# 64x32 instead of 64x64 TensorE tiles in the chunked recurrence of a gated linear attention with an MLP behind it

## The chip, the cores and the metric

The kernel runs on one core of one Trainium2 chip. The metric is the device time of one launch in microseconds (us). Before the change three runs gave 178.33, 179.40 and 180.58 us; the median is 179.4 us. The engines are TensorE (PE in the profile; PEld are its weight loads), VectorE (DVE), ScalarE (ACT), GpSimd (POOL) and SyncE (SP), which only issues DMAs here.

## The reference

Inputs are q, k, v and alpha of shape (4 batches, 8 heads, 768 steps, 48 features), and two weights, 384 x 2048 and 2048 x 384.

```python
for t in range(S):                       # per batch and head, state is D x D
    state = alpha[:, :, t, :, None] * state + np.einsum('bhd,bhe->bhde', k[:, :, t], v[:, :, t])
    y[:, :, t] = np.einsum('bhd,bhde->bhe', q[:, :, t], state)
x = y.transpose(0, 2, 1, 3).reshape(B * S, H * D)      # 3072 x 384
h = x @ w_in
r = np.maximum(h, 0.0)
out = (r * r) @ w_out                                  # 3072 x 384
```

## The kernel before, in words

**Tiling.** The 768 steps of a batch are cut into three pairs of chunks, 256 steps a pair and 128 a chunk, so there are 12 pairs, g = 0 to 11. On the partitions a chunk lies as 64 rows of two neighbouring steps (index i or n). Features are padded from 48 to 64 a head, and heads go two by two, so a head pair fills 128 partitions of a transposed tile.

**Stages of a pair.** (1) `loads`: four transfers, alpha, k, q, v, into RAW. (2) `decay` (`decay_half` for the first two pairs): logarithms on ScalarE, running sums over the chunk on TensorE (L502 and L504; L541 and L546 for the first two pairs), exponentials, and the scaled k and q in bf16 (QKS) on VectorE. `values` casts v to bf16 (VBF), on GpSimd for the first two pairs. (3) `turned`: QKS is transposed to QKT, on TensorE for the first three pairs, by a DMA on SyncE's queue from there on. (4) `scores` (L634): 32 matmuls of 64x64 tiles, 128 columns each, in two halves of 16; VectorE multiplies them by the causal mask into PMB (L644, four instructions). (5) `carry` (L663): the end states of the pair's chunks, k times v, 32 matmuls of 48 columns (16 in the last pair of a batch, where one chunk is enough). VectorE and GpSimd make the state behind each chunk of it (L678, L681, L683, tile SBF). (6) `mixed` (L702): the values, 48 matmuls of 128 columns (PMB times VBF), and the part that comes from the states, in two halves of 12 (6 in the first pair of a batch). The second half waits until the first has left the array (`drain`), because both add into the same bank from other row groups. ScalarE copies the result to XT (L740). (7) `up` (L757): eight units of 6 matmuls, 256 columns each; ScalarE applies the relu (L761), VectorE squares (L763). (8) `down` (L781): eight groups of 4 matmuls with 384 columns, then a copy by ScalarE (L788) and an output DMA; the last chunk goes in two halves of columns (L801, L806).

**Tiles on TensorE.** `scores`, `carry` and `mixed` use a quarter of the array for a matmul: 64 rows (the chunk's row half or the head's half) by 64 columns (which half of the output partitions). In `mixed` the 384 output features are cut into six groups of 64; each of the 8 heads with 48 features touches one or two of them, which gives the list `shares` of 12 pieces. The order of the matmuls goes round the four quarters.

**Order.** Nothing is issued in program order. `Program.add` records each operation with an engine, an estimated duration in ns, what it reads and writes, and a due time `at`; `form` is the tile shape of TensorE work. `order` plays the program through with these durations and gives each engine the ready operation with the earliest due time; TensorE prefers work of the form that it is in, and a change of form is reckoned with 95 ns. `fill` puts warm-up matmuls (L770) into idle time of TensorE that this plan shows ahead of the first down matmul. `plan` places semaphore waits. The due times are 2 g plus an offset for each stage, from the tables OFF, EARLY (pairs 0 and 1) and MID (pair 2). SyncE holds the loads, the transposes and the outputs in one queue, in the order of the plan; GpSimd's queue holds the casts of the first two pairs, the weights' DMAs (four for w_in, which wait for alpha of pair 1, then four for w_out) and the states' second step.

## Time and profile before

| what | value |
|---|---|
| median of three runs | 179.4 us (178.33 to 180.58) |
| span of the profiled execution | 177.0 us |
| granted TensorE clock | 0.999 |
| L757 up, PE | 576 matmuls, busy 74.0 us |
| L781 down, PE | 368 matmuls, busy 71.4 us |
| L702 mixed, values, PE | 576 matmuls of 64x64 tiles, busy 10.4 us |
| L702 mixed, from the states, PE | 240 matmuls, busy 8.6 us |
| L634 scores, PE | 384 matmuls, busy 8.0 us |
| L663 end states, PE | 320 matmuls, busy 5.5 us |
| L770 warm-up, PE | 22 matmuls, busy 7.6 us |

The span runs from the first to the last instruction of the profiled execution; the runs' times hold 2.4 us more at the median. Busy time of a matmul reaches to its modelled end, and these ends overlap with the next starts, so the price of a group is read from start to start. A row of the timeline has start, duration to the end of its last instruction, engine, line, operation, tiles, shape, count and, in brackets, idle time of the engine before it with what ended it. A row of a windows table has the window, its length, busy time and count of each engine (where TensorE alone was asked for, only its own), the granted clock, the mean share of the 16 DMA engines and GB/s. Of the DMA queues, `q8 instruction` are transfers of instructions.

### The profile page before, as it was taken

How to read it: one execution, taken by the hardware profiler on the slowest of the kernel's cores; microseconds unless marked ns; L12 is line 12 of the kernel's file. 1: busy time of each engine (PE TensorE's matmuls, PEld its weight loads, DVE VectorE, ACT ScalarE, POOL GpSimd, SP SyncE). 2: the span in 40 equal slices, each digit the busy share in tenths (PEclk: the TensorE clock that was granted, in tenths of full speed). 3: DMA queues.
4: the chain of work that ended last, by engine and by line, in shares of the span. 5: the costliest groups of instructions: out<-in, count | busy, mean ns of one | idle time of the engine just before them, and what ended most of it. 6: DMA issues, size and time to landing. Idle time of an engine off the chain costs nothing.

```text
span 177.0 us, 6054 instructions
## 1 busy us (share of the span) xinstructions
PE 169.4 (96%) x2648; PEld 123.8 (70%) x2648; DVE 117.1 (66%) x251; ACT 116.8 (66%) x235; POOL 19.3 (11%) x35
## 2 busy tenths in 40 slices
PE   7989699999999989999999999999999999999993
PEld 2656568776666877787777777777777777767772
DVE  7998534599889797993896694875663952732400
ACT  4764376695894878796989779756566645455531
POOL 4179400001100201001002001001001010000000
PEclk9999999999999999999999999999999999999999
DMA  5999999899999999999899999831701331101112
GB/s 137 308 298 171 193 204 216 228 302 275 269 216 298 198 285 240 277 248 240 222 325 214 282 232 279 202 84 50 167 4 44 92 75 44 48 4 52 37 44 93
DMA packets 75994, 31.85 MB, mean 180 GB/s; under 512 B 69184, under 2 KB 75968, under 8 KB 75968
## 3 DMA queue, kind: packets, MB, share of 16 engines
q1 hardware_dynamic: 72256, 28.32, 64.1%
q0 software_dynamic: 3712, 3.15, 11.7%
q8 instruction: 21, 0.34, 0.8%
q14 instruction: 5, 0.04, 0.1%
HBM read 25.17 MB, written 4.72 MB: 169 GB/s over the span
## 4 chain that ended last, share of the span: by engine, by line
PE 76%; DMA 14%; SPq 4%; ACT 3%; issue 2%
PE psH L757 32%; PE psO L781 30%; PE psG L702 6%; DMA qkt<-qks 4%; DMA win<-in_moe_w_in_dram 4%; SPq L474 4%; DMA raw<-in_v_dram 3%; DMA raw<-in_alpha_dram 3%; PE psG L634 3%; PE psO L801 1%; PE psG L663 1%; ACT xt L740 1%; ACT rr L761 1%; PE psG L502 1%; PE psG L574 1%
## 5 line engine op out<-in xcount | busy, mean ns | idle before, releaser
L761 ACT ACTIVATE rr<-psH 128x512 bf16<-128x512 f32 x96 | 56.6, 598 | 35.9 <-PE psH L757 34.9
L757 PE MATMUL psH<-xt,win 128*128 128x256 bf16 x576 | 74.0, 273 | 0.7 <-DMA win<-in_moe_w_in_dram 0.3
L781 PE MATMUL psO<-wout,gt 128*128 128x384 bf16 x368 | 71.4, 326 | 0.0
L757 PEld LDWEIGHTS psH<-xt,win 128*128 128x128 bf16 x576 | 54.5, 98 | 14.4 <-ACT rr L761 1.4
L763 DVE TENSOR_TENSOR gt<-rr 128x512 bf16<-128x512 bf16 x96 | 39.9, 423 | 36.0 <-ACT rr L761 35.4
L781 PEld LDWEIGHTS psO<-wout,gt 128*128 128x128 bf16 x368 | 34.5, 98 | 17.1
L644 DVE TENSOR_TENSOR pm<-psG,mask 128x512 bf16<-128x512 f32 x48 | 30.8, 685 | 1.6 <-PE psG L634 1.5
L523 DVE TENSOR_TENSOR qks<-raw,asb 128x768 bf16<-128x768 f32 x20 | 18.6, 956 | 6.5 <-ACT asb L512 6.5
L683 POOL TENSOR_TENSOR sbf<-ust,acp 128x192 bf16<-128x192 f32 x16 | 9.3, 579 | 119.1 <-DVE ust L681 119.0
L740 ACT ACTIVATE xt<-psG 128x384 bf16<-128x384 f32 x24 | 13.1, 597 | 5.7 <-PE psG L702 5.7
L788 ACT ACTIVATE osb<-psO 128x384 f32<-128x384 f32 x23 | 11.3, 493 | 4.8 <-PE psO L781 4.3
L493 DVE TENSOR_TENSOR raw<-raw 128x384 f32<-128x384 f32 x20 | 11.0, 555 | 2.4 <-DMA raw<-in_alpha_dram 1.7
L512 ACT ACTIVATE asb<-psG 128x384 bf16<-128x384 f32 x20 | 9.8, 490 | 1.6 <-PE psG L504 1.4
L702 PEld LDWEIGHTS psG<-pm,vbf 64*64 64x64 bf16 x576 | 8.4, 107 | 2.8 <-issue 1.4
L702 PE MATMUL psG<-pm,vbf 64*64 64x128 bf16 x576 | 10.4, 218 | 0.0
L702 PE MATMUL psG<-qkt,sbf 64*64 64x128 bf16 x240 | 8.6, 220 | 1.4 <-issue 1.4
L485 ACT ACTIVATE vbf<-raw 128x768 bf16<-128x768 f32 x10 | 8.4, 843 | 1.1 <-DMA raw<-in_v_dram 1.0
L634 PEld LDWEIGHTS psG<-qkt 64*64 64x64 bf16 x384 | 5.9, 106 | 4.4 <-issue 1.4
L770 PE MATMUL psO<-warm 128*128 128x512 bf16 x22 | 7.6, 472 | 1.1 <-DVE warm L391 1.1
L634 PE MATMUL psG<-qkt 64*64 64x128 bf16 x384 | 8.0, 219 | 0.5 <-DMA qkt<-qks 0.4
L681 DVE TENSOR_TENSOR ust<-psG,sbf 128x192 f32<-128x192 f32 x15 | 5.3, 356 | 2.8 <-POOL sbf L683 2.3
L702 PEld LDWEIGHTS psG<-qkt,sbf 64*64 64x64 bf16 x240 | 5.2, 106 | 2.7 <-issue 2.6
(65 smaller groups left out, 99.9 us busy)
## 6 DMA issues: line engine op xcount, KB each, us to landing
raw<-in_k_dram SPq DMA_DIRECT2D x12, 384.0 KB, 5.0
raw<-in_q_dram SPq DMA_DIRECT2D x12, 384.0 KB, 5.6
raw<-in_v_dram SPq DMA_DIRECT2D x12, 384.0 KB, 5.4
out_dram<-osb SPq DMA_DIRECT2D x23, 192.0 KB, 3.5
raw<-in_alpha_dram SPq DMA_DIRECT2D x11, 384.0 KB, 5.2
win<-in_moe_w_in_dram POOLq DMA_DIRECT2D x4, 384.0 KB, 8.7
wout<-in_moe_w_out_dram POOLq DMA_DIRECT2D x4, 384.0 KB, 12.3
raw<-in_alpha_dram SPq DMA_DIRECT2D x2, 192.0 KB, 2.7
```

The costliest lines, as they stand in the source:

```text
L493: add("DVE", lambda e: e.tensor_tensor(dst, a0, a1, ALU.mult), 470, at_, reads=reads, writes=writes)
L512: add("ACT", lambda act, z=z: act.activation(ASB[a][:, z, 0, :], ps[:, 0:HD], AF.Exp, scale=2.0 * z - 1.0), 372, at + 0.04 + 0.02 * z, rea ...
L523: add("DVE", lambda dve, z=z, decays=decays: dve.tensor_tensor(QKS[x][:, z, :, :, 0:D], both(r, z), decays, ALU.mult), 870, at + 0.05 + 0. ...
L634: last = pe.matmul(banks[i, j // 2][0][64 * c:64 * c + 64, col:col + 128].rearrange("p (a b) -> p a b", a=2), QKT[t][64 * i:64 * i + 64, 0 ...
L644: add("DVE", lambda dve, i=i, X=X, ps=ps: dve.tensor_tensor(PMB[m][:, i, 2 * X:2 * X + 2].rearrange("p j n s -> p j (n s)"), ps[:].rearran ...
L702: last = pe.matmul(o, lhsT, rhs, start=(c, n % 2) not in begun, stop=True, skip_group_check=True)
L740: add("ACT", lambda act, ps=ps, base=base: act.activation(XT[:, :, base:base + C].rearrange("f k (p i) -> f k i p", i=2), ps[:, 0:HD].rear ...
L757: last = pe.matmul(ps[:, f * TW:(f + 1) * TW], WIN[:, kt, fj * 128:(fj + 1) * 128], XT[:, kt, g * TW:(g + 1) * TW], start=(kt == 0), stop= ...
L761: add("ACT", lambda act: act.activation(RR[r][:], ps[:], AF.Relu), 480, at, reads=[key], writes=[key, ("rr", r)])
L763: add("DVE", lambda dve: dve.tensor_tensor(gt[:, 2 * u:2 * u + 2, :], rr, rr, ALU.mult), 340, at, reads=[("rr", r)], writes=[("gt", g % NG ...
L781: last = pe.matmul(ps[:, 0:DM], GT[g % NGT][:, fj, tt * 128:(tt + 1) * 128], WOUT[:, fj, :], start=(fj == 0), stop=(fj == FT - 1))
L788: add("ACT", lambda act: act.activation(OSB[o][:], ps[:, 0:DM], AF.Copy), 372, at, reads=[key], writes=[key, ("osb", o)])
```

## The change

Values, the part from the states, and the end states use 64x32 tiles: 64 rows by 32 columns, eight to the array. The 384 output features are cut into twelve groups of 32 (16 pieces in `shares`), so the values take 64 matmuls, each half of the part from the states 16 (8), and the end states 64 (32). Scores keep 64x64. The planner's durations change with it, it gets a model of the arrival of instructions (blocks of 256; the next block comes 4300 ns after a block's start in the first 30 us, and 2700 ns after a point 48 instructions ahead of it later), and the offsets of the stages are new, with a table each for pairs 0 and 1. With these the order on every engine is another. TensorE gets 3246 matmuls where it had 2648; the other engines' instructions are the same in number and kind.

In the new order TensorE has, in the early part: pair 0's decay and transposes, half of its scores, its end states, pair 1's decay, the other half of the scores, 11 warm-up matmuls, pair 0's values and first half from the states, pair 1's end states, the second half, a warm-up matmul, pair 1's transposes, two up units, half of pair 1's scores, an up unit, the other half, three up units, pair 1's values. Before, pair 1's scores stood ahead of the first up unit and its end states behind the second. On VectorE two of pair 0's four masks stand behind pair 1's scaled k and q; before, all four stood ahead. On SyncE, from pair 3 on, a transpose stands ahead of the next pair's alpha load, and the first output ahead of k, q and v of pair 4.

```diff
+CFG = {'OFF': {'decay': -4.835, 'turned': -3.891, 'scores0': -2.056, 'scores1': -2.206,
+               'carry': -3.164, 'mixed': -1.691, 'up': -1.026},
...
+ 'CW': 32}
...
+    OTHER = 20
+    BLOCK, QUEUE, FETCH, FETCH_LATE, BUSY_UNTIL = 256, 48, 4300.0, 2700.0, 30000.0
...
+            if e == "PE" and op.mm:
+                each, began = op.work / op.mm, t
+                for i in range(op.mm):
+                    x = count + i
+                    lead = 0 if t < self.BUSY_UNTIL else self.QUEUE
+                    if (x + lead) % self.BLOCK == 0:
+                        b = (x + lead) // self.BLOCK + 1
+                        came[b] = t + i * each + (self.FETCH if t < self.BUSY_UNTIL else self.FETCH_LATE)
+                    if x % self.BLOCK == 0 and came.get(x // self.BLOCK, 0.0) > t + i * each:
+                        late = came[x // self.BLOCK] - t - i * each
...
+        W = CFG.get("CW", 64)
+
         def mm(pe):
             for j in range(NP):
                 for n in range(2):
-                    for i in range(2):
-                        for c in chunks:
-                            last = pe.matmul(banks[c][0][64 * i:64 * i + 64, j * D:(j + 1) * D],
-                                             QKS[x][64 * c:64 * c + 64, 0, n, 2 * j + i, :],
+                    for d in range(0, 64, W):
+                        for i in range(2):
+                            for c in chunks:
+                                last = pe.matmul(banks[c][0][64 * i + d:64 * i + d + W, j * D:(j + 1) * D],
+                                                 QKS[x][64 * c:64 * c + 64, 0, n, 2 * j + i, d:d + W],
...
-        add("PE", mm, 170 + 150 * len(chunks), at, reads=[("qks", x, 0, X) for X in range(2)] + [("vbf", vb)],
-            writes=[b[1] for b in banks], form=64)
+        add("PE", mm, 250, at, reads=[("qks", x, 0, X) for X in range(2)] + [("vbf", vb)],
+            writes=[b[1] for b in banks], form=W, mm=1024 // W * len(chunks))
...
-    shares = [(h, n, 64 * n - D * h) for h in range(H) for n in range(2 * KT) if -64 < 64 * n - D * h < D]
+    NG = HD // 32
+    shares = [(h, n, 32 * n - D * h) for h in range(H) for n in range(NG) if -32 < 32 * n - D * h < D]
...
-            o = banks[c][0][64 * (n % 2):64 * (n % 2) + 64, n // 2 * 128:n // 2 * 128 + 128]
+            o = banks[c][0][32 * (n % 4):32 * (n % 4) + 32, n // 4 * 128:n // 4 * 128 + 128]
...
-            order = [[s for s in shares if s[1] % 2 == col] for col in range(2)]
-            for y in range(2 * KT):
+            order = [[s for s in shares if s[1] % 4 == col] for col in range(4)]
+            for y in range(4):
                 for i in range(2):
-                    for col in range(2):
+                    for col in range(4):
                         h, n, off = order[col][y]
...
-        add("PE", mm, 640, at, reads=[("vbf", vb)] + [("pm", m, i, X) for i in range(2) for X in range(2)],
-            writes=[b[1] for b in banks], form=64)
+        add("PE", mm, 455, at, reads=[("vbf", vb)] + [("pm", m, i, X) for i in range(2) for X in range(2)],
+            writes=[b[1] for b in banks], form=32, mm=64)
...
-        o = EARLY if g < FIRST else MID if g < TURN else OFF
+        o = EARLY[g] if g < FIRST else MID if g < TURN else OFF
```

More of the change, by code (lines that the diff above doesn't have):

```diff
@@ L1 @@
 import heapq
+CFG = {'OFF': {'decay': -4.835,
+         'turned': -3.891,
+         'scores0': -2.056,
+         'scores1': -2.206,
+         'carry': -3.164,
+         'mixed': -1.691,
+         'up': -1.026},
+ 'MID': {'decay': -4.897,
+         'turned': -3.845,
+         'scores0': -3.102,
+         'scores1': -3.012,
+         'carry': -3.319,
+         'mixed': -1.513,
+         'up': -1.423},
+ 'E0': {'decay': -6.997,
+        'turned': -5.74,
+        'scores0': -5.321,
+        'scores1': -3.593,
+        'carry': -3.833,
+        'mixed': -3.228,
+        'up': -1.919},
+ 'E1': {'decay': -6.326,
+        'turned': -4.764,
+        'scores0': -3.707,
+        'scores1': -3.627,
+        'carry': -5.044,
+        'mixed': -2.649,
+        'up': -2.169},
+ 'CW': 32}
 import concourse.bass as bass
@@ L25, in __init__ @@
         self.count = None
+        self.mm = 0
         self.signal = False
@@ L52, in add @@
     def add(self, eng, fn, work, at, reads=(), writes=(), dma=None, nbytes=0, rate=0.0, behind=None, form=None,
-            drain=None):
+            drain=None, mm=0):
         op = Op(len(self.ops), eng, fn, work, at, dma, nbytes, rate)
@@ L79, in add @@
         op.form = form
+        op.mm = 2 * mm
         self.ops.append(op)
@@ L94, in order @@
         self.sequence = []
+        self.stalls = []
         known = dict.fromkeys((o.n for o in self.ops), 0.0)
@@ L150, in order @@
         form = None
+        count, came = 64 + self.OTHER, {}
         while left:
@@ L193, in order @@
                 form = op.form
+            if e == "PE" and op.mm:
[8 more added lines that the diff above has]
+                        late = came[x // self.BLOCK] - t - i * each
+                        self.stalls.append((t + i * each, late))
+                        if i:
+                            op.work += late
+                            each = op.work / op.mm
+                        else:
+                            t += late
+                count += op.mm
             free[e] = t + op.work
@@ L434, in bass_gla_recurrent__then__act_relu_squared_kernel @@
     OPENS = {2: 5}
+    RUNS, OPENS = CFG.get("RUNS", RUNS), CFG.get("OPENS", OPENS)
     pieces = [(w, n) for w in ("in", "out") for n in range(WH)]
@@ L506, in sums @@
             return last
-        add("PE", sums, 265, at + 0.02, reads=lab + ["hinc"], writes=[key])
+        add("PE", sums, 265, at + 0.02, reads=lab + ["hinc"], writes=[key], mm=1 + NP)
         add("ACT", lambda act: act.activation(heads(RO[o_][:]), odd, AF.Ln), 412, at + 0.03,
@@ L549, in sums @@
             return last
-        add("PE", sums, 430, at + 0.01, reads=[("lab", l, X), "hinc", "hexc"], writes=[key])
+        add("PE", sums, 430, at + 0.01, reads=[("lab", l, X), "hinc", "hexc"], writes=[key], mm=8)
         for z in range(2):
@@ L575, in tr @@
                 return last
-            add("PE", tr, 450, at + 0.02 * z, reads=[("qks", x, z, X) for X in range(2)] + ["ident"], writes=[key])
+            add("PE", tr, 450, at + 0.02 * z, reads=[("qks", x, z, X) for X in range(2)] + ["ident"], writes=[key], mm=8)
             dst = QKT[t][:, z].rearrange("p i j s -> p (i j s)")
@@ L608, in tr @@
                 return last
-            add("PE", tr, 225, at + 0.02 * z, reads=[("qks", x, z, X), "ident"], writes=[key])
+            add("PE", tr, 225, at + 0.02 * z, reads=[("qks", x, z, X), "ident"], writes=[key], mm=4)
             if g > 0 and z == 0:
@@ L640, in scores @@
         add("PE", mm, 112 * len(js), at, reads=[("qkt", t, z, X) for z in range(2) for X in halves],
-            writes=[b[1] for b in banks.values()], form=64)
+            writes=[b[1] for b in banks.values()], form=64, mm=8 * len(js))
         mask = bass.AP(tensor=MASK, offset=0, ap=[[256, 128], [0, 2], [1, 256]])
@@ L660, in mm @@
                 for n in range(2):
-                    for i in range(2):
-                        for c in chunks:
-                            last = pe.matmul(banks[c][0][64 * i:64 * i + 64, j * D:(j + 1) * D],
-                                             QKS[x][64 * c:64 * c + 64, 0, n, 2 * j + i, :],
-                                             VBF[vb][64 * c:64 * c + 64, n, 2 * j + i, 0:D],
-                                             start=n == 0, stop=n == 1)
-            return last
-        add("PE", mm, 170 + 150 * len(chunks), at, reads=[("qks", x, 0, X) for X in range(2)] + [("vbf", vb)],
-            writes=[b[1] for b in banks], form=64)
+                    for d in range(0, 64, W):
[3 more added lines that the diff above has]
+                                                 QKS[x][64 * c:64 * c + 64, 0, n, 2 * j + i, d:d + W],
+                                                 VBF[vb][64 * c:64 * c + 64, n, 2 * j + i, 0:D],
+                                                 start=n == 0, stop=n == 1)
+            return last
+        add("PE", mm, 250, at, reads=[("qks", x, 0, X) for X in range(2)] + [("vbf", vb)],
+            writes=[b[1] for b in banks], form=W, mm=1024 // W * len(chunks))
         for c in chunks:
@@ L698, in one @@
         def one(pe, c, n, lhsT, rhs):
-            o = banks[c][0][64 * (n % 2):64 * (n % 2) + 64, n // 2 * 128:n // 2 * 128 + 128]
+            o = banks[c][0][32 * (n % 4):32 * (n % 4) + 32, n // 4 * 128:n // 4 * 128 + 128]
             if len(rhs.shape) == 3:
                 o = o.rearrange("p (a b) -> p a b", a=2)
-            last = pe.matmul(o, lhsT, rhs, start=(c, n % 2) not in begun, stop=True, skip_group_check=True)
-            begun.add((c, n % 2))
+            last = pe.matmul(o, lhsT, rhs, start=(c, n % 4) not in begun, stop=True, skip_group_check=True)
+            begun.add((c, n % 4))
             return last
         def before(pe, swap):
-            order = [[[s for s in shares if s[0] % 2 == i and s[1] % 2 == col] for col in range(2)] for i in range(2)]
-            for y in range(KT):
-                for col in range(2):
+            order = [[[s for s in shares if s[0] % 2 == i and s[1] % 4 == col] for col in range(4)] for i in range(2)]
+            for y in range(2):
+                for col in range(4):
                     for i in range(2):
@@ L715, in before @@
                             at_ = D + PAD * (h // 2) + off
-                            last = one(pe, c, n, SBF[(2 * g + c) % NS][64 * i:64 * i + 64, at_:at_ + 64],
+                            last = one(pe, c, n, SBF[(2 * g + c) % NS][64 * i:64 * i + 64, at_:at_ + 32],
                                        QKT[t][64 * i:64 * i + 64, 1, :, h // 2, 64 * c:64 * c + 64])
@@ L720, in mm @@
         def mm(pe):
-            order = [[s for s in shares if s[1] % 2 == col] for col in range(2)]
-            for y in range(2 * KT):
+            order = [[s for s in shares if s[1] % 4 == col] for col in range(4)]
+            for y in range(4):
                 for i in range(2):
-                    for col in range(2):
+                    for col in range(4):
                         h, n, off = order[col][y]
@@ L727, in mm @@
                         for c in range(2):
-                            last = one(pe, c, n, flat[64 * c:64 * c + 64, PAD * h + off:PAD * h + off + 64],
+                            last = one(pe, c, n, flat[64 * c:64 * c + 64, PAD * h + off:PAD * h + off + 32],
                                        PMB[m][64 * c:64 * c + 64, h % 2, h // 2, i, :])
             return last
-        add("PE", mm, 640, at, reads=[("vbf", vb)] + [("pm", m, i, X) for i in range(2) for X in range(2)],
-            writes=[b[1] for b in banks], form=64)
+        add("PE", mm, 455, at, reads=[("vbf", vb)] + [("pm", m, i, X) for i in range(2) for X in range(2)],
+            writes=[b[1] for b in banks], form=32, mm=64)
         reads = [("qkt", t, 1, X) for X in range(2)] + [("sbf", (2 * g + c) % NS) for c in chunks]
         keys = [banks[c][1] for c in chunks]
-        first = add("PE", lambda pe: before(pe, 0), 80 * len(chunks), at + 0.004, reads=reads, writes=keys, form=64)
-        add("PE", lambda pe: before(pe, 1), 80 * len(chunks), at + 0.008, reads=reads, writes=keys, form=64, drain=first)
+        first = add("PE", lambda pe: before(pe, 0), 57 * len(chunks), at + 0.004, reads=reads, writes=keys, form=32, mm=8 * len(chunks))
+        add("PE", lambda pe: before(pe, 1), 57 * len(chunks), at + 0.008, reads=reads, writes=keys, form=32, drain=first, mm=8 * len(chunks))
         for c in range(2):
@@ L759, in mm @@
             return last
-        add("PE", mm, 655, at, reads=[("xt", 2 * g), ("xt", 2 * g + 1), ("win", 2 * u * WH // FT)], writes=[key])
+        add("PE", mm, 655, at, reads=[("xt", 2 * g), ("xt", 2 * g + 1), ("win", 2 * u * WH // FT)], writes=[key], mm=6)
         add("ACT", lambda act: act.activation(RR[r][:], ps[:], AF.Relu), 480, at, reads=[key], writes=[key, ("rr", r)])
@@ L771, in busy @@
         return last
-    add("PE", lambda pe: busy(pe, 7), 2950, -6, reads=["warm"], writes=[("psO", i) for i in range(NPO)])
+    add("PE", lambda pe: busy(pe, 7), 2950, -6, reads=["warm"], writes=[("psO", i) for i in range(NPO)], mm=7)
     def down(g, tt, p, at):
@@ L784, in down @@
         op = add("PE", mm, 650, at, reads=[("gt", g % NGT, f) for f in range(4 * p, 4 * p + 4)] + [("wout", 4 * p * WH // FT)],
-                 writes=[key])
+                 writes=[key], mm=4)
         downs.append(op)
@@ L804, in last_down @@
                 add("PE", mm, 330, at + c + 0.25 * p, reads=[("gt", (G - 1) % NGT, f) for f in range(4 * p, 4 * p + 4)]
-                    + [("wout", 4 * p * WH // FT)], writes=[key])
+                    + [("wout", 4 * p * WH // FT)], writes=[key], mm=4)
             add("ACT", lambda act, ps=ps, o=o: act.activation(OSB[o][:, 0:HW], ps[:, 0:HW], AF.Copy), 215, at + c + 0.75,
@@ L814, in bass_gla_recurrent__then__act_relu_squared_kernel @@
     MID = dict(decay=-4.614, turned=-4.532, scores0=-3.642, scores1=-3.538, carry=-4.386, mixed=-1.189, up=-1.023)
-    stages = [(2 * r[0] + (EARLY["decay"] + 0.5 if run else 0.96 - 2 * NRAW), lambda at, run=run: weights(at, run))
+    for d, name in ((OFF, "OFF"), (EARLY, "EARLY"), (MID, "MID")):
+        d.update(CFG.get(name, {}))
+    EARLY = [{**EARLY, **CFG.get("E%d" % i, {})} for i in range(FIRST)]
+    stages = [(2 * r[0] + (CFG["WAT"][run] if "WAT" in CFG else EARLY[1]["decay"] + 0.5 if run else 0.96 - 2 * NRAW), lambda at, run=run: weights(at, run))
               for run, r in enumerate(RUNS)]
     for g in range(G):
-        o = EARLY if g < FIRST else MID if g < TURN else OFF
+        o = EARLY[g] if g < FIRST else MID if g < TURN else OFF
         stages.append((2 * g - 2 * NRAW + 0.95, lambda at, g=g: loads(g, at)))
```

## The prediction

> **What bounds the kernel now.** I read the page's busy shares and its chain first, then the timeline of TensorE (PE) in a steady stretch, then PE's idle time.

> ```profile
> span 177.0 us, 6054 instructions
> PE 169.4 (96%) x2648; PEld 123.8 (70%) x2648; DVE 117.1 (66%) x251; ACT 116.8 (66%) x235; POOL 19.3 (11%) x35
> PE 76%; DMA 14%; SPq 4%; ACT 3%; issue 2%
> ...
> 174.03 0.33 ACT osb L806
> ```

> PE is busy for 96% of the span, no other engine for more than 66%, and the chain is mostly PE. So the end is PE's last matmul (174.0 us, where the last copy starts), and a step is worth what it adds to PE's stream or takes from it. Rows of matmuls give their price by the distance between starts, since the modelled ends overlap:

> ```profile
> 75.49 1.47 PE L757 MATMUL psH<-xt,win 128*128 128x256 bf16 x12
> 76.80 0.81 PE L781 MATMUL psO<-wout,gt 128*128 128x384 bf16 x4
> 77.45 1.47 PE L757 MATMUL psH<-xt,win 128*128 128x256 bf16 x12
> 78.86 0.86 PE L702 MATMUL psG<-pm,vbf 64*64 64x128 bf16 x48
> 79.55 0.34 PE L702 MATMUL psG<-qkt,sbf 64*64 64x128 bf16 x12
> 79.72 0.42 PE L663 MATMUL psG<-vbf,qks 64*64 64x48 bf16 x32
> 79.97 0.37 PE L702 MATMUL psG<-qkt,sbf 64*64 64x128 bf16 x12
> 80.27 0.99 PE L781 MATMUL psO<-wout,gt 128*128 128x384 bf16 x5
> ```

> Twelve up matmuls cost 1.31 (75.49 to 76.80), four down 0.65. Before a tiled group twelve cost 1.41, so entering 64x64 tiles costs 0.10; the last half of the states takes 0.30 where the first takes 0.17, so leaving costs 0.13. The tiled groups run in rounds of four matmuls, one a tile: values 48 matmuls, 12 rounds, 0.69 us, 0.0575 a round; a half of the states 12 matmuls, 3 rounds, 0.17, 0.056 a round; end states 32 matmuls, 8 rounds, 0.25, 0.031 a round.

> The early stretch holds the largest idle time of PE:

> ```profile
> 12.85 0.86 PE L702 MATMUL psG<-pm,vbf 64*64 64x128 bf16 x48
> ...
> 16.79 1.48 PE L757 MATMUL psH<-xt,win 128*128 128x256 bf16 x12 [0.34 <-DMA win<-in_moe_w_in_dram]
> ...
> 20.09 0.31 PE L702 MATMUL psG<-qkt,sbf 64*64 64x128 bf16 x8
> 21.83 0.25 PE L702 MATMUL psG<-qkt,sbf 64*64 64x128 bf16 x4 [1.44 <-issue]
> ```

> The 1.44 us fall inside one group of 12, whose wait stands ahead of its first matmul; nothing that the profile shows was awaited. I read it as instructions that had not come. The rows for this:

> ```profile
> 0.00:10.00 10.00, 8.56 (x110) 4.72 (x110) 8.24 (x32) 5.75 (x12) 2.74 (x10) 1.00 0.88 234
> 10.00:20.00 10.00, 9.15 (x229) 6.52 (x229) 9.01 (x18) 5.85 (x13) 8.79 (x11) 1.00 1.17 213
> ...
> q8 instruction: 21, 0.34, 0.8%
> ...
> q8 instruction: 1, 0.02, 5.6%
> ```

> The last row is of 19.3 to 20.4 us. On the page, 21 transfers of 16 KB serve 2648 matmuls and as many weight loads: 252 instructions each, so I take blocks of 256, or 128 matmuls. The stall comes after 110 + 229 + 8 = 347 matmuls, and one transfer ran just ahead of its end. Further block starts should then stand near matmuls 859, 1243 and 2395 (347 + 4, + 7 and + 16 times 128). PE's counts to 57.95, 79.72 and 152.20 us, and the transfers around:

> ```profile
> 0.00:57.95 57.95, 53.89 (x854) 1.00 1.07 240
> 0.00:79.72 79.72, 75.21 (x1240) 1.00 1.08 242
> 0.00:152.20 152.20, 147.63 (x2390) 1.00 0.87 201
> ...
> q1 hardware_dynamic: 2186, 0.64, 104.8%
> ...
> q8 instruction: 1, 0.02, 5.4%
> ...
> q1 hardware_dynamic: 892, 0.32, 67.3%
> ...
> q8 instruction: 1, 0.02, 5.8%
> ...
> DMA packets 0, 0.00 MB, mean 0 GB/s; under 512 B 0, under 2 KB 0, under 8 KB 0
> ...
> q8 instruction: 1, 0.02, 5.3%
> ```

> The DMA rows are of 57.9 to 61.1 us (data only), 61.1 to 62.2, 79.8 to 81.9 (data only), 81.9 to 82.9, 150.4 to 151.4 (nothing) and 151.4 to 152.5. So at each block start one block is asked for, and I read it as the next one: the sequencer holds the block it reads and one more. In the quiet part the transfer starts a little before PE reaches the block's start (the sequencer reads ahead; I take 16 matmuls, an estimate, 0 to 32 possible), and 5.3% of 16 engines in 1.1 us are 0.93 us of transfer. Sixteen matmuls before that start PE is at about 150.4 us, so asking to arrival takes at least 2.0 us (151.4 + 0.93); I take 2.2. While the loads fill the DMA engines (share 1.07 to 58 us) it starts 3.2 us (after 57.9) or 2.2 us (after 79.7) behind PE: 4.2 and, with the 0.2 us of sixteen matmuls, 3.3 us. A block lasts 94.25 us / 1536 x 128 = 7.9 us on average, so only the one is late.

> **The change part by part.**

> *Values and states.* A 64x32 tile is half as wide, so eight run at once if they run as four do. Values: 64 matmuls in 8 rounds of 0.0575, 0.46 for 0.69. A half of the states: 16 in 2 rounds, 0.11 for 0.17 (with one chunk, 8 on four tiles, the same). Sum per pair -0.23 - 0.11 = -0.34, twelve pairs -4.1 us, all on PE's path.

> *End states.* 64 matmuls in 8 rounds of 0.031: 0.25 as now. Bounds: rounds as short as their 48 columns ask (0.056 x 48/128 = 0.021) give -0.08 a pair, four at a time +0.25. I take 0, the round's row.

> *Changes of form.* 62 in the new order, 60 in the old; scores keep 64x64 but stand apart from 64x32 groups but for up, down or warm-up matmuls. One round trip more, +0.2.

> *The other engines* run the same instructions in another order. Waits for them cost PE little (0.34 for the weights above), and I leave that sum; bounds -1 to +1. On SyncE the transposes move ahead of the next pair's alpha load and one output ahead of the fifth pair's k, q and v: these come later by the output's wait, and cover is the time to that pair's decay.

> *The start.* Values of the first pair need all four masks, which now stand on VectorE partly behind the second pair's products:

> ```profile
> 9.20 2.48 DVE L644 TENSOR_TENSOR pm<-psG,mask 128x512 bf16<-128x512 f32 x4 [0.23 <-PE psG L634]
> ...
> 12.59 2.12 DVE L555 TENSOR_TENSOR qks<-raw,asb 128x384 bf16<-128x384 f32 x3
> ...
> 14.35 1.04 POOL L483 CAST vbf<-raw 128x768 bf16<-128x768 f32 x1
> ```

> The same work ends at about the same 14.7, with a release 15.2, where values started at 12.85. The second pair's end states now stand before the first up matmul and need the cast (15.4): no later wait. Then values 0.46, states 0.11, end states 0.25, a warm-up matmul 0.2, sixteen transposes 0.9, changes 0.3: up starts at 17.4 instead of 16.79, and its 12 matmuls end at 18.8.

> There, at matmul 349 of the new order, the third block starts. It was asked for at block two's start, inside the values, at 15.6; now that is 14.9. It came at 21.83; delays in that stretch are of the DMA engines (share 1.17), so I take 22.0. Bounds: 18.8 (no stall) and 22.7. From there on PE has left what it had left at 21.83 in this kernel, 152.2 us, and: values 11 x 0.46 against 10 x 0.69, -1.8; halves of states 19 x 0.11 against 18.3 x 0.17, -1.0; an up group +0.66, 27 scores +0.4, two round trips +0.5, a warm-up matmul -0.2: 150.7. PE's end without further stalls: 172.7, against 174.0.

> *Blocks in the dense groups.* 3246 matmuls make 25 blocks for 21. Values, states and end states of a pair were 104 matmuls, less than a block, and are 160 now, in about a microsecond. In the new order block starts fall at 730 and 858, 986 and 1114, 1241 and 1369, 1496 and 1624, 1751 and 1879, 2262 and 2390, 2517 and 2645, with little between. From asking (16 matmuls ahead) to need, the prices above give 1.7 us (52 values 0.37, two halves 0.22, down with its changes 0.88, 56 end states 0.22), then 1.1 to 2.3 (by how far the sequencer reads into the down group ahead), 3.4, 3.1, 3.0, 1.6 and 1.0 to 2.1. The first five lie before 107 us, where loads run: at 3.3, the low loaded row, stalls of 1.6, 1.6, 0, 0.2 and 0.3. The last two at 2.2: 0.6 and 0.7. Sum 5.0. Bounds: at 2.0 everywhere and 24 ahead 0.7; at 4.2 loaded and 3 quiet some 10.

> *Sum.* PE's end 172.7 + 5.0 = 177.7, 3.7 later than 174.0; span 180.7. The median of the runs, 179.4, is 2.4 above the profiled span; with the same distance 183.1 us.

> **The rivals.**

> *Instructions are never late.* For it: the 1.44 us happen once, at the most loaded place. Then block three does not stall (18.8), and PE ends at 18.8 + 150.7 = 169.5, 4.5 earlier: 174.9 us. It holds if a new block reaches PE in under a microsecond, or if more than one is held ahead. Against it: transfers begin at the block starts, one each, and take 0.93 us alone. [...]

> *Late but nearly covered.* Requests go out 24 or more matmuls ahead and take 2.0 us: 0.7 of stalls, block three at 20.5, PE's end 171.9, 177.3 us: within 2%. Speaks for it: the quiet transfer begins before PE is there. Against it: the loaded row.

> *Tiles of 64x32 do not run eight at once* but four in a round: per pair +0.23 values, +0.11 states, +0.25 end states, 0.59 instead of -0.34, 0.93 x 12 = 11 us over the forecast, 194. The rounds of four with four tiles speak against it; no row shows eight.

> **How the numbers follow.** Forecast (late blocks cost more than the tiles save; 179 to 188) 0.62, never late 0.18, nearly covered 0.13, no eight at once 0.07. Likeliest 183.1. The range 175.5 to 188 leaves out the last rival, a part of the first, and stalls past 10 us. With 2% as what a measurement here can tell, under 175.8 is two thirds of the first rival, 0.12; over 183.0 half or more of the forecast and the last rival, 0.43; the rest 0.45.

> **What would show it.** Values x64 in 0.46, halves x16 in 0.11 and end states x64 in 0.25 by starts show the first steps; 0.9 for values the last rival. First up at 17.4. Idle PE put down to "issue" at matmuls near 349, 858, 1114, 2390 and 2645, each after a short block, and about 25 instruction transfers, show the blocks; PE without such idle time proves the forecast wrong.

## The result, and the profile after

The changed kernel takes 194.35 us (median of four runs, 190.96 to 195.84) against 178.87 us for the kernel before beside it: ratio 1.072, 95% interval 1.060 to 1.083, so some 13 us slower by the ratio. Medians here and below are of all runs, ratios of the fast runs alone (of the changed kernel 193.29 and 190.96 us). The forecast was 183.1 us, with 175.5 to 188 as the range: the direction was the one that it held likeliest, the size was wrong. The profiled execution took 193.29 us; in it the last matmul starts at 188.75 us, in that of the kernel before at 173.75, and the account further down explains these 15.0 us.

The page of the changed kernel, and the row of the last copy from its timeline:

```profile
span 191.4 us, 7259 instructions
PE 173.8 (91%) x3246; PEld 125.7 (66%) x3246; DVE 117.0 (61%) x251; ACT 117.8 (62%) x235; POOL 20.0 (10%) x35
...
q8 instruction: 25, 0.41, 0.8%
...
PE 83%; issue 7%; DVE 3%; DMA 3%; ACT 2%; SPq 1%
...
189.04 0.33 ACT L864 ACTIVATE osb<-psO 128x192 f32<-128x192 f32 x1 [0.99 <-PE psO L859]
```

PE still bounds the kernel, but it stands idle for 9% of the span where it was 4%, "issue" holds 7% of the chain where it held 2%, and there are 25 instruction transfers where there were 21. Who PE waited for, in total, times and longest, in the changed kernel:

```profile
PE psO L839 <- issue: 3.6, 3, 1.5
PE psH L815 <- issue: 2.9, 2, 1.7
PE psG L760 <- issue: 2.9, 1, 2.9
PE psG L688 <- issue: 1.9, 1, 1.9
PE psG L720 <- issue: 1.2, 1, 1.2
```

and in the kernel before:

```profile
PE psG L702 <- issue: 1.4, 1, 1.4
```

That is 12.5 us in eight stops against 1.4 in one. The stops in the timeline of the changed kernel (the number in brackets is idle time, from the modelled end of the matmul ahead):

```profile
19.08 0.30 PE L688 MATMUL psG<-qkt 64*64 64x128 bf16 x5
21.26 0.36 PE L688 MATMUL psG<-qkt 64*64 64x128 bf16 x11 [1.88 <-issue]
...
23.25 3.48 PE L815 MATMUL psH<-xt,win 128*128 128x256 bf16 x18
26.66 0.74 PE L760 MATMUL psG<-pm,vbf 64*32 64x128 bf16 x64
...
47.84 0.67 PE L720 MATMUL psG<-vbf,qks 64*32 64x48 bf16 x56
49.72 0.22 PE L720 MATMUL psG<-vbf,qks 64*32 64x48 bf16 x8 [1.21 <-issue]
...
60.89 0.30 PE L760 MATMUL psG<-qkt,sbf 64*32 64x128 bf16 x7
64.06 0.28 PE L760 MATMUL psG<-qkt,sbf 64*32 64x128 bf16 x1 [2.87 <-issue]
64.28 2.74 PE L839 MATMUL psO<-wout,gt 128*128 128x384 bf16 x8
66.81 0.58 PE L815 MATMUL psH<-xt,win 128*128 128x256 bf16 x3
...
88.87 0.49 PE L815 MATMUL psH<-xt,win 128*128 128x256 bf16 x3
90.53 0.49 PE L815 MATMUL psH<-xt,win 128*128 128x256 bf16 x3 [1.17 <-issue]
```

Each stop cuts a group in two (5 and 11 of 16, 56 and 8 of 64, 7 and 1 of 8, 3 and 3 of 6), so no wait of the program is awaited there. Counted from the first, the matmuls that come late are numbers 349, 858, 1114, 1624, 1879, 2135, 2390, 2645 and 2900: the block starts of the prediction. Lateness beyond the usual distance from start to start, in us (the sum is of the unrounded values; the forecast for 349 is 22.0 less 18.8):

| block start | 349 | 858 | 1114 | 1369 | 1624 | 1879 | 2135 | 2390 | 2645 | 2900 | sum |
|---|---|---|---|---|---|---|---|---|---|---|---|
| forecast | 3.2 | 1.6 | 1.6 | 0 | 0.2 | 0.3 | - | 0.6 | 0.7 | - | 8.2 |
| measured | 2.0 | 1.3 | 3.0 | 0.2 | 1.3 | 1.7 | 1.0 | 1.4 | 1.9 | 0.5 | 14.4 |

The transfer for the stop at 64.06 runs from 61.60 to 62.61; the DMA queues from 61.5 to 62.7 us:

```profile
q1 hardware_dynamic: 315, 0.12, 51.4%
q8 instruction: 1, 0.02, 5.3%
```

PE goes on 1.45 us after that transfer has ended. At all these stops it is 1.2 to 1.6 us (1.4 on average), and at the one stop of the kernel before 1.48 (20.35 to 21.83).

The dense groups themselves, by the distance of their starts, in an undisturbed pair of one chunk and one of two:

```profile
114.28 0.74 PE L760 MATMUL psG<-pm,vbf 64*32 64x128 bf16 x64
114.80 0.35 PE L760 MATMUL psG<-qkt,sbf 64*32 64x128 bf16 x16
114.94 0.46 PE L720 MATMUL psG<-vbf,qks 64*32 64x48 bf16 x32
115.23 0.35 PE L760 MATMUL psG<-qkt,sbf 64*32 64x128 bf16 x16
...
127.35 0.73 PE L760 MATMUL psG<-pm,vbf 64*32 64x128 bf16 x64
127.87 0.35 PE L760 MATMUL psG<-qkt,sbf 64*32 64x128 bf16 x16
128.00 0.74 PE L720 MATMUL psG<-vbf,qks 64*32 64x48 bf16 x64
128.56 0.35 PE L760 MATMUL psG<-qkt,sbf 64*32 64x128 bf16 x16
```

Values take 0.52 us (forecast 0.46), a half of the states 0.13 to 0.14 (0.11), 64 end states 0.56 (0.25).

### The profile page after: what moved, and what is told of

It is laid out like the page before. It is cut to its first block, busy times and chain, and to the rows that moved or that the text cites. A ratio compares the mean times of both kernels' runs of the same rounds, so it can differ in the third digit from the quotient of the medians.

```text
span 191.4 us, 7259 instructions
## 1 busy us (share of the span) xinstructions
PE 173.8 (91%) x3246; PEld 125.7 (66%) x3246; DVE 117.0 (61%) x251; ACT 117.8 (62%) x235; POOL 20.0 (10%) x35
## 3 DMA queue, kind: packets, MB, share of 16 engines
HBM read 25.17 MB, written 4.72 MB: 156 GB/s over the span
## 4 chain that ended last, share of the span: by engine, by line
PE 83%; issue 7%; DVE 3%; DMA 3%; ACT 2%; SPq 1%
PE psH L815 33%; PE psO L839 32%; PE psG L760 6%; PE psG L688 4%; PE psG L720 3%; DMA raw<-in_q_dram 3%; DVE qks L609 2%; PE psO L859 1%; DVE pm L698 1%; PE psG L556 1%; SPq L528 1%; PE psO L828 1%; ACT xt L798 1%; PE psG L660 1%; ACT rr L819 0%
## 5 line engine op out<-in xcount | busy, mean ns | idle before, releaser
L815 PE MATMUL psH<-xt,win 128*128 128x256 bf16 x576 | 78.1, 276 | 3.3 <-issue 2.9
L839 PE MATMUL psO<-wout,gt 128*128 128x384 bf16 x368 | 74.6, 331 | 3.6 <-issue 3.6
L815 PEld LDWEIGHTS psH<-xt,win 128*128 128x128 bf16 x576 | 55.5, 99 | 18.5 <-issue 4.1
L740 POOL TENSOR_TENSOR sbf<-ust,acp 128x192 bf16<-128x192 f32 x16 | 10.2, 640 | 131.3 <-DVE ust L738 131.3
L760 PE MATMUL psG<-qkt,sbf 64*32 64x128 bf16 x320 | 8.3, 222 | 2.9 <-issue 2.9
L688 PE MATMUL psG<-qkt 64*64 64x128 bf16 x384 | 8.5, 223 | 2.2 <-issue 1.9
L760 PEld LDWEIGHTS psG<-pm,vbf 64*32 64x32 bf16 x768 | 7.2, 90 | 4.3 <-DVE pm L698 1.6
L828 PE MATMUL psO<-warm 128*128 128x512 bf16 x28 | 8.9, 443 | 1.1 <-DVE warm L444 1.1
L760 PE MATMUL psG<-pm,vbf 64*32 64x128 bf16 x768 | 8.8, 221 | 0.7 <-DVE pm L698 0.7
L720 PE MATMUL psG<-vbf,qks 64*32 64x48 bf16 x576 | 7.3, 189 | 1.2 <-issue 1.2
```

Source lines behind the costliest of these rows:

```text
L688: last = pe.matmul(banks[i, j // 2][0][64 * c:64 * c + 64, col:col + 128].rearrange("p (a b) -> p a b", a=2), QKT[t][64 * i:64 * i + 64, 0 ...
L720: last = pe.matmul(banks[c][0][64 * i + d:64 * i + d + W, j * D:(j + 1) * D], QKS[x][64 * c:64 * c + 64, 0, n, 2 * j + i, d:d + W], VBF[vb ...
L760: last = pe.matmul(o, lhsT, rhs, start=(c, n % 4) not in begun, stop=True, skip_group_check=True)
L815: last = pe.matmul(ps[:, f * TW:(f + 1) * TW], WIN[:, kt, fj * 128:(fj + 1) * 128], XT[:, kt, g * TW:(g + 1) * TW], start=(kt == 0), stop= ...
L839: last = pe.matmul(ps[:, 0:DM], GT[g % NGT][:, fj, tt * 128:(tt + 1) * 128], WOUT[:, fj, :], start=(fj == 0), stop=(fj == FT - 1))
```

## The experiments

Two theories stood against each other for the stops. *Late blocks*: PE holds the block that it reads and one more, and stops where 128 matmuls pass before the next has come. *Dense groups*: eight tiles at once, or many small matmuls, stall by themselves (weight loads, banks, the drain), wherever blocks start. For the prices of the groups a third question was open: the array, or the rate at which instructions come.

**Tiles alone.** Before with 64x32 tiles in all three groups, old planner and offsets:

```diff
-                    for i in range(2):
+                    for d in range(0, 64, 32):
+                        for i in range(2):
...
-    shares = [(h, n, 64 * n - D * h) for h in range(H) for n in range(2 * KT) if -64 < 64 * n - D * h < D]
+    shares = [(h, n, 32 * n - D * h) for h in range(H) for n in range(HD // 32) if -32 < 32 * n - D * h < D]
```

> The kernel before with all 64x32 tiles of the change, its own offsets and planner. Late blocks (theory): values, states and end states of a pair stand together again as 128 or 160 matmuls, so about ten blocks of 128 matmuls pass in 1 to 3 us; at 4 to 4.6 us from 16 matmuls ahead to arrival while loads run and 3.3 to 3.6 after, 17 to 22 us of stalls, each at a block's start (every 128 matmuls from 347), and 190 to 200 us. New offsets to blame (rival): 178 to 181. Narrow tiles themselves to blame (rival): the groups take 0.06 us more a pair, 179 to 181.

201.23 us, ratio 1.100 (1.087 to 1.112). Lateness at block starts sums to 21.2 us, in eleven places, 127 or 128 matmuls apart or a multiple of that. The sum is read from the kept trace, an execution of 203.59 us. The tiles bring the whole loss; the new offsets take some of it back.

**Order alone.** The changed kernel with 64x64 tiles everywhere:

```diff
- 'CW': 32}
+ 'CW': 64}
...
-    shares = [(h, n, 32 * n - D * h) for h in range(H) for n in range(NG) if -32 < 32 * n - D * h < D]
+    shares = [(h, n, 64 * n - D * h) for h in range(H) for n in range(2 * KT) if -64 < 64 * n - D * h < D]
```

> The changed kernel with its offsets and planner but 64x64 tiles everywhere. Late blocks: a pair's tiled groups are 104 matmuls again, no block is passed in under 5 us after the first three, no stall there, 177 to 182 us. New offsets to blame: 192 to 196. Narrow tiles to blame: as before, 178 to 180.

178.99 us, ratio 0.999 (0.995 to 1.002), no stop at a block start. The offsets by themselves change nothing that can be measured.

**Only the end states wide.** The changed kernel with `'CW': 64` alone: values and states in 64x32 tiles, end states in 64x64, so a pair issues 128 small matmuls and not 160.

> The changed kernel with end states in 64x64 tiles (32 matmuls, another form, so that the planner puts them apart from the values). Late blocks: 0.6 to 2 us of stalls behind 24 us, 178 to 183. Offsets to blame: 192 to 196. Narrow tiles to blame: the values and states keep them, 184 to 190.

179.29 us, ratio 0.997 (0.993 to 1.001), lateness at block starts 0.4 us in all. So the loss comes with the narrow end states, and the narrow values and states alone gain nothing that can be measured. The order changes here too: the planner puts end states in another form apart from the values, and in the trace an up group (103.69 us) stands between the two halves of the states (103.41 and 104.45). Fewer matmuls and a looser order are not told apart by this run.

**Blocks moved by 59 matmuls.** This tells the two theories apart: the order is that of the changed kernel, and only the count ahead of it differs.

```diff
-    add("PE", lambda pe: busy(pe, 7), 2950, -6, reads=["warm"], writes=[("psO", i) for i in range(NPO)], mm=7)
+    def shifted(pe):
+        busy(pe, 2)
+        for i in range(64):
+            last = pe.matmul(psO[i % NPO][:, 0:2], WARM[:], WARM[:, 0:2])
+        return last
+    add("PE", shifted, 2950, -6, reads=["warm"], writes=[("psO", i) for i in range(NPO)], mm=7)
```

> The changed kernel with every instruction in the same order, but the first seven warm-up matmuls replaced by two of them and 64 of two columns, which moves all block starts to 59 matmuls earlier in the work. Late blocks: the stalls at 858, 1114, 1624, 1879, 2135, 2390, 2645 and 2900 are gone, only some at 1055 and 1565 (numbers of the changed kernel), 2 to 4 us in all behind 24 us, and 178 to 184 us. Offsets or tiles to blame: the order and the tiles are the same, 193 to 196.

180.98 us, ratio 1.009 (1.004 to 1.014). The ratio was 1.072, so some 11 of the 13 us go with 59 more matmuls on zeros at the start. Lateness at block starts is 3.7 us, at 290, 1310, 1565 and 2331 in the numbers of the changed kernel, each 59 below a block start; at 858, 1114 and the others nothing is left. Dense groups that stall by themselves are ruled out.

**Blocks moved by 92 matmuls**, where nearly all block starts lie outside the dense groups with a long block ahead (four warm-up matmuls and 95 of two columns in place of seven):

> The changed kernel, all groups in 64x32 tiles, with three of the seven first warm-up matmuls replaced by 95 matmuls of two columns: all else keeps its order, and each block of 128 matmuls starts 92 matmuls earlier in it, which puts nearly all block starts outside the dense groups with a long block ahead of each. Late instruction blocks: idle time at block starts in all under 3 us (14 in the changed kernel), PE's last matmul at 174 to 177 us, 179 to 182.5 us. If the dense groups stall by themselves, wherever blocks start: idle time in the same groups as in the changed kernel, 193 to 195 us.

182.30 us, ratio 1.013 (1.009 to 1.017). The same place of the order as the first stop with end states above, in this kernel:

```profile
49.21 0.30 PE L760 MATMUL psG<-qkt,sbf 64*32 64x128 bf16 x16
49.34 0.73 PE L720 MATMUL psG<-vbf,qks 64*32 64x48 bf16 x64
50.00 0.82 PE L845 MATMUL psO<-wout,gt 128*128 128x384 bf16 x4
```

The 64 end states run through, and the down group stands 0.66 us behind their start (2.03 in the changed kernel, 47.84 to 49.87). Lateness at block starts is 2.0 us, as expected; PE's last matmul starts at 176.9, as expected. But the first up matmul starts at 21.0 and not at 17.7, so the time is less good than the stops allow. From the first up matmul to the last matmul it is 155.8 us, 153.8 without the stops (in the later run with the added matmuls in 64x32 tiles 157.2, and 154.0 without its 3.2 us of stops). The same for the kernel before is 157.0, or 155.4 without its stop.

**The kernel before, moved by the same 92 matmuls:**

> The kernel before with the same 95 two-column matmuls for three of its first warm-up matmuls: its block start at matmul 347, where PE stood idle for 1.6 us, moves to matmul 255 of the old count. Late instruction blocks: that idle time goes and nothing takes its place, 177.3 to 178.2 us against 179 (ratio 0.990 to 0.996). If the idle time belongs to that half of the states and not to the block start: it stays, 179.

178.86 us, ratio 0.997 (0.993 to 1.000). The idle time at the block start is gone, as expected, but the first up matmul starts at 18.57 instead of 16.79: 1.8 us lost at the start for 1.6 saved, so the expected time was missed. From the first up matmul to the last it is 155.6 us here, with no stop.

**The added matmuls made cheap.** For both kernels, the 95 in 64x32 tiles:

```diff
-            last = pe.matmul(psO[i % NPO][:, 0:2], WARM[:], WARM[:, 0:2])
+            d, c = 32 * (i // 2 % 4), 64 * (i % 2)
+            last = pe.matmul(psO[i % 2][d:d + 32, 0:2], WARM[c:c + 64, 0:32], WARM[c:c + 64, 0:2])
```

> As the shifted kernel before, but the 95 added matmuls are in 64x32 tiles, which should take 8 to 10 ns each where the 128x128 ones took 27 (2.58 us, 1.3 us longer than the three warm-up matmuls that they stand for). Late instruction blocks and a start as early as that of the kernel before: first up matmul at 16.6 to 17.0 us, no idle time at a block start, PE's last matmul at 172.0 to 172.8 us, 177.2 to 178 us, ratio 0.989 to 0.994. If the later start of the shifted kernel was due to the block starts themselves and not to the slow pads: first up at 18.3 or later and a ratio near 0.997 again.

> The changed kernel with the same 95 matmuls in 64x32 tiles: nearly all block starts outside the dense groups, and the start as early as in the changed kernel (first up at 17.5 to 17.9 us instead of 21.0). PE's body then takes what it took in the shifted kernel, 153.8 us without stalls, and some 2 us of stalls while the loads run: last matmul at 173 to 174.5 us, 178.3 to 180 us, ratio 0.994 to 1.004. If the tiles saved what the prediction gave them (0.34 us a pair, 4.1 in all, on a stall-free stream): last matmul at 170 us, 175 us.

179.14 us, ratio 0.995 (0.991 to 1.000), for the kernel before, and 181.07 us, ratio 1.010 (1.006 to 1.013), for the changed one. The start was still late, first up at 18.62 and 18.68. Why is seen in the early windows of the second (5.69 to 7.78 us), and of the changed kernel (5.72 to 6.80), and in the rows of the five warm-up matmuls that stand there:

```profile
5.69:7.78 2.09, 2.09 (x11) 0.71 (x9) 1.08 (x3) 1.52 (x5) 0.00 (x0) 1.00 1.13 307
...
5.69 2.29 PE L828 MATMUL psO<-warm 128*128 128x512 bf16 x5
```

```profile
5.72:6.80 1.08, 1.08 (x11) 1.00 1.17 325
...
5.72 1.24 PE L828 MATMUL psO<-warm 128*128 128x512 bf16 x5
```

The same five matmuls take 2.09 us in place of 1.08. The granted clock of 1.00 in both rows says nothing here: the clock records kept with the traces begin at 8.67 us in this run and at 5.55 in the changed kernel, and ahead of them the column reads 1.00. From start to start a warm-up matmul takes 0.43 us ahead of the first record and 0.22 behind it, so TensorE ran at half pace until then. The theory that only the slow added matmuls delayed the start fell. That the three large warm-up matmuls fewer delayed it is not shown either: the run under "The price of small matmuls" has the unchanged start of the kernel before, with all seven, and there the five were as slow, and the first up matmul started at 18.73:

```profile
6.32 2.29 PE L770 MATMUL psO<-warm 128*128 128x512 bf16 x5
```

**All warm-up matmuls kept, 92 added where PE is idle:** behind the first end states in the kernel before, behind the second half of the scores in the changed one.

```diff
+            for i in range(92 if g == 0 else 0):
+                d, s = 32 * (i // 2 % 4), 64 * (i % 2)
+                pe.matmul(psO[i % 2][d:d + 32, 0:2], WARM[s:s + 64, 0:32], WARM[s:s + 64, 0:2])
             return last
```

> The kernel before with all its warm-up matmuls and 92 added matmuls of two columns in 64x32 tiles behind the first end states, where TensorE otherwise waits 0.73 us for ScalarE. They should take some 0.77 us there (8.3 ns each), so the start is no later than in the kernel before, and the block start at matmul 347 moves to 255. Late instruction blocks: no idle time at a block start, first up at 16.8 to 17.0 us, PE's last matmul at 172.0 to 172.8 us, 177.3 to 178.2 us, ratio 0.989 to 0.994. If TensorE's early matmuls do not gain by this because the loads set the pace there: last matmul at 173.7 us and ratio 1.

> The changed kernel with all its warm-up matmuls and the same 92 added matmuls behind the second pair of scores, where TensorE otherwise waits 0.74 us ahead of the first values. Start as in the changed kernel: first up at 17.6 to 18.0 us. Stall-free body 153.8 us as the shifted kernels had it, and 1 to 3 us of idle time at block starts while the loads run: last matmul at 172.5 to 174.8 us, 178 to 180.5 us, ratio 0.992 to 1.004; so no gain over the kernel before with its block shifted. If the tiles saved 4.1 us on a stall-free stream: last matmul at 170 us, 175 us.

179.77 us, ratio 1.005 (1.001 to 1.009), and 184.29 us, ratio 1.031 (1.024 to 1.037): both missed. Rows of the second:

```profile
12.07 0.61 PE L695 MATMUL psO<-warm 64*32 64x2 bf16 x62
14.74 0.28 PE L695 MATMUL psO<-warm 64*32 64x2 bf16 x30 [2.05 <-issue]
...
18.07 0.25 PE L723 MATMUL psG<-vbf,qks 64*32 64x48 bf16 x11
20.84 0.59 PE L723 MATMUL psG<-vbf,qks 64*32 64x48 bf16 x50 [2.52 <-issue]
```

The expectation had overlooked that 92 small matmuls in 0.8 us are themselves a short block: PE stops inside the added matmuls, which read nothing but zeros and wait for nobody, at number 222, and again 127 matmuls later (and once more at number 1369, with 2.11 us idle). It is the plainest sight of a late block in the study. The kernel before stops at numbers 221 and 348 in the same way, 2.1 us in two idle times for the 1.4 that were to go.

**The price of small matmuls.** The kernel before with groups of 96 small matmuls on zeros behind its end, each run of small ones behind large ones:

```diff
+        def small(pe, w=w, cols=cols):
+            for i in range(96):
+                c, d = i % 2, w * (i // 2 % (128 // w))
+                last = pe.matmul(psG[c][d:d + w, 0:cols], WARM[64 * c:64 * c + 64, d:d + w], WARM[64 * c:64 * c + 64, 0:cols])
```

> The kernel before, with six groups of 96 small matmuls on zeros added behind its last matmul, each behind 24 large ones (128x512); so it takes some 36 us longer by design, and only the distances between starts count. Groups: 64x32 tiles with 128, 48 and 16 columns, then 64x64 tiles with 128, 48 and 16 columns. If an issue rate sets the dense groups (one weight load and matmul in 8.3 ns once those that were queued ahead are used up): the last 50 of each group come 8.3 ns apart for 64x32 at 128, 48 and 16 columns and for 64x64 at 48 and 16 columns, all five alike, and 14.4 ns for 64x64 at 128 columns. If the array sets them (the rounds of the prediction): 64x32 at 128 columns 7.2 ns, at 48 columns 3.9 and at 16 columns no more than that, 64x64 at 48 columns 7.8.

Two of the pairs were put directly one behind the other (x192 below). Rows of the timeline, and from the same trace the distances between starts:

```profile
181.20 1.77 PE L853 MATMUL psG<-warm 64*32 64x128 bf16 x192
...
193.37 0.91 PE L853 MATMUL psG<-warm 64*32 64x16 bf16 x96
...
199.49 2.31 PE L853 MATMUL psG<-warm 64*64 64x128 bf16 x192
...
212.20 0.94 PE L853 MATMUL psG<-warm 64*64 64x16 bf16 x96
```

| ns from start to start | matmuls 8 to 24 | last 50 |
|---|---|---|
| 64x32, 128 columns, behind large | 7.00 | 8.32 |
| 64x32, 48 columns, behind 64x32 | 8.38 | 8.34 |
| 64x32, 16 columns, behind large | 3.38 | 8.34 |
| 64x64, 128 columns, behind large | 13.94 | 13.52 |
| 64x64, 48 columns, behind 64x64 | 7.94 | 8.26 |
| 64x64, 16 columns, behind large | 8.00 | 7.80 |

As the issue rate asks: 128, 48 and 16 columns in 64x32 tiles cost the same in the long run, 8.3 ns. The 64x64 rows with 48 and 16 columns, 7.8 to 8.3, do not decide, since their round of four takes about 32 ns, 8 a matmul, from the first two dozen on. Behind large matmuls the first two dozen in 64x32 tiles come at the array's pace: 8 x 7.00 ns is 0.056 us, the forecast's round with eight tiles. So eight tiles did run at once there (7.00 ns against 13.94 with four); behind the two dozen something else sets the pace, and whether that is the reading of instructions or the loading of weights is left open.

## Why the prediction was wrong

**What bounds the kernel; the start.** Right. PE's last matmul sets the end. Values of the first pair came at 15.03 (forecast 15.2), the first up matmul at 17.68 (17.4).

**Where blocks start.** Right: blocks of 128 matmuls (the late ones stand 127 or 128 apart, or a multiple of that), one fetched ahead (PE is at number 986 at 59.70 us, the next transfer runs from 61.60 to 62.61, and number 1114 waits for it until 64.06), and the seven starts named; two more that cost time, 2135 and 2900, were not on its list. Moving the count by 59 moved the stops by 59.

**"Sum 5.0" for the dense blocks: the first step that failed, by its size.** These blocks cost 12.4 us, past even its bound of some 10; 1.5 of them are the two starts that it did not list. (The stop at 349 went the other way, 2.0 us for 3.2.) The time from asking to need was about right, the time from asking to having was not: the forecast took 3.3 us while loads run and 2.2 in the quiet part. Counted from 16 matmuls ahead of the block start ahead, as the forecast did (its estimate; no run shows when a block is asked for), the late blocks took 3.5 to 5.1 us (858, 1114, 1624, 1879, 2135) and 3.2 to 4.0 (2390, 2645, 2900). Of the difference 1.4 us are the time from the end of the transfer to the next matmul: the forecast let PE go on when the transfer ended, though its own row with 1.44 us of idle time, held against that transfer's end at 20.35, shows 1.48 us between the two. With that alone its 2.2 would have been 3.6 and its 3.3 4.7, both inside what was measured.

The rival "instructions are never late" is ruled out: ten of the 25 blocks cost 0.2 to 3.0 us each.

**"-0.34 a pair" for the tiles: the second.** Priced by rounds of the array, which held only for the first two dozen 64x32 matmuls behind large ones (7.00 ns apart). After these each matmul with its weight load took 8.3 ns: 64 x 8.3 is 0.53, and values took 0.52; end states have 64 matmuls where they had 32, and took 0.56 for 0.25, past even the bound of +0.25 that stood for four at a time. Over the kernel, by distances of starts with the changes of form in them and without stops: values 8.4 us before and 6.3 after, states 5.5 and 4.9, end states 3.7 (a wait of 0.7 for ScalarE taken off) and 5.9. That is about -0.5 us, not -4.1. The rival "not eight at once" had the loss of the end states about right, for a reason that the runs do not bear out.

**A term that was missing: the clock.** The two longest stops, with 1.88 and 2.87 us of idle time, are each followed by a stretch at a granted clock of 0.50. Windows of PE in the changed kernel, the two with a granted clock of 0.50 and one of 1.00:

```profile
22.61:26.02 3.41, 3.34 (x30) 0.50 1.31 204
63.57:66.98 3.41, 2.92 (x10) 0.50 1.11 306
...
67.20:70.60 3.40, 3.40 (x32) 1.00 0.29 92
```

Eighteen up matmuls take 3.41 us there (23.25 to 26.66), by the prediction's price of 0.109 each 1.97; eight down matmuls 2.53 (64.28 to 66.81) for 1.31. With the scores ahead of the first (0.2) the two stretches cost some 2.9 us. The length of a stop alone does not decide it. In the traces the granted clock changes only on a grid of 3.41 us (the stretches between changes are 3.41 us or multiples of it; in the changed kernel it changes at 22.61, 26.03, 63.57 and 66.99, up to the last matmul), and the change goes with PE's busy time in one window of that grid. Three windows of the changed kernel, and one of the kernel moved by 59 matmuls:

```profile
19.20:22.61 3.41, 1.30 (x22) 1.00 1.25 200
60.16:63.57 3.41, 1.03 (x102) 1.00 0.97 217
142.08:145.49 3.41, 1.67 (x132) 1.00 0.02 5
...
15.26:18.68 3.42, 1.66 (x145) 1.00 1.11 161
```

The first, the second and the fourth are followed by 0.50, the third is not. All eight half-clock stretches that begin between the first clock record and the last matmul in the traces follow a window with 1.75 us or more of idle time, about half of it; no window at full clock with 1.74 us or less was followed by one. So a stop of 1.13 us, with other idle time beside it, brought one in the kernel moved by 59 matmuls, and a stop of 2.05 us that lay across two windows brought none in the changed kernel with 92 added matmuls.

**The account.** Stall-free, the changed order takes 153.8 us from the first up matmul (the run moved by 92). 17.7 + 153.8 + 14.4 (stops) + 2.9 (half clock) = 188.8; PE's last matmul starts at 188.75. For the kernel before 16.8 + 155.4 + 1.6 = 173.8 holds by construction, since the 155.4 come from the same trace; the check is the kernel before moved by 92 matmuls, which had no stop and took 155.6. So of the 15.0 us, 12.8 are late blocks, 2.9 the clock behind them, and all the rest together, start, tiles and order, -0.7. The start is 0.9 of that and the tiles about -0.5; the other -1.1 is what is left over, and no run takes it apart. The forecast had late blocks at 8.2, the clock at nothing, and, on the other side, tiles at -4.1.

**Left open.** What fills the 1.4 us between a transfer's end and the next matmul, and whether the 8.3 ns are the rate of reading instructions or of loading weights: each small matmul here has a load of its own. So is what delayed the start of the kernels with added matmuls, and how much of the spread between runs is the clock: of 82 runs of the kernel before beside the experiments, 41 with a granted clock of 0.998 or more took 179.0 us at the median and 40 with about 0.99 took 180.2, and no trace of the latter is kept. No version here beats the kernel before by more than half a per cent (0.995, the kernel before with its block moved); of the versions with 64x32 tiles throughout, the best was the one moved by 59 matmuls, 1.009.

## What to carry to other kernels

Count instructions as well as work: here TensorE stopped for up to 3.0 us where 128 matmuls with their loads passed in less than the next block took (3.5 to 5.1 us while loads ran, 3.2 to 4.0 later, counted as above), and where the block starts fell decided it: 59 and 92 matmuls added ahead moved the stops. A smaller tile gained nothing from the array once the array's time for a matmul, divided by the tiles at work, was under the 8.3 ns that each matmul with its load took here; from there the number of matmuls set the price (values 64 x 8.3 ns for 48 x 14.4, still a gain; end states 64 x 8.3 for 32 x 7.8, a loss). When a late transfer is priced, measure to the first instruction that used it, not to the transfer's end: here 1.2 to 1.6 us lay between the two.
